# Where the first seed copies and the exponential's table load stand, and how far ahead seeds are loaded, in a two-headed SSM and attention kernel

## The chip, the cores and the metric

One Trainium2 chip, one core. The metric is the device time of one execution in microseconds, and the comparison is between the kernel before and the kernel after the change.

## The reference

Two independent heads on sequences of 2048 positions and width 448 are computed and put side by side. Head A is a long convolution with a diagonal state-space kernel; head B is softmax attention with 16 heads of width 28.

```python
# A: S4D convolution
dt = exp(log_dt);  A = -exp(log_A_real) + 1j * A_imag
C = (C_real + 1j * C_imag) * dt[:, None]
P = exp((A * dt[:, None])[:, :, None] * pos)      # 448 x 256 x 2048
K = 2 * einsum("dn,dnl->dl", C, P).real
a = irfft(rfft(u_t, 2L) * rfft(K, 2L))[:L] + u * D_skip
# B: attention, 16 heads of 28
q, k, v = split(x @ wqkv)
p = softmax(q @ k.T * 28 ** -0.5)
b = (p @ v).reshape(S, D) @ wo
out = concatenate([a, b], -1)
```

## The kernel before

The kernel has a prologue, a loop of 256 steps and a tail.

The **prologue** projects x to q, k and v with TensorE (each evacuated into a high and a low part by ACT and DVE, tile `hl`, and written to DRAM) and works out "seeds" for the state-space kernel: low powers of the complex exponentials, from which all 2048 positions are later built by multiplication. Seeds need ACT's sine and exponential functions, which lie in different tables, so the program has table loads (`ACT_TABLE_LOAD` in the profile) between them. Seeds are written to DRAM (`sd`). In the prologue a planner is free to order the instructions of each engine. At its end the scores' maxima of attention unit 0 are found, in 16 groups of 4 (`max_mm`, line 173).

One group of `max_mm` takes four products of 128 x 512 scores on TensorE (tiles `pm`). The first is passed through a relu on ACT (tile `rl`), the second is joined with it on DVE (custom instruction, output `rl`), the third and fourth are reduced on DVE (output `mx`). `max_end` and `max_put` (lines 198 and 206) turn the maxima over and write them as two further rows into the tile `qhat`, through which they come into the scores.

The **loop** runs over 16 units (4 groups of 4 heads, 4 chunks of 512 queries each) with 16 key tiles each. A step (`ORDER`, line 34) holds four score products with their exponentials on ACT (`s_mm`, tiles `pss` and `p`), the previous step's four products with v (`pv_step`, tile `po`), one group of maxima for a coming unit (19 steps ahead: 16 and `LEAD` = 3), and pieces of the convolution. In the loop and from line 861 on, every engine's instructions, SP's DMA requests among them, stay in the order in which the program writes them.

The pieces of the convolution that matter here are the 56 **blocks** of 8 channels, one each 3.5 steps. For a block b:

- `load_sd(b)` (line 615) loads its seeds into a tile `sdb`, 128 x 672 floats;
- `k_seeds(b)` (line 619) copies them on ACT, at its first call into the tile `e`, at its second into `g`;
- `k_start(b)` copies further factors into `zg`; `e_power` (line 633) then doubles the powers in `e` in nine instructions on POOL, `g_powers` those in `g` on DVE;
- `k_mm` (line 674) multiplies e by g on TensorE, four steps after the block began.

The next load is issued by `k_next` (line 987) once a block's powers have all been written into the program. Between prologue and loop stand the loads and copies for block 0 and then the first `LEAD` groups of maxima for unit 1.

Of the kernel before, what the change touches and what calls it, by code (L numbers as in the profile page):

```python
# [8 lines left out]
F32 = mybir.dt.float32  # L9
F32R = mybir.dt.float32r  # L10
I32 = mybir.dt.int32
AF = mybir.ActivationFunctionType
# [38 lines left out]
NB = D // 8  # L51
# [7 lines left out]
SDF = F_Z + 18 * 16  # L59
# [31 lines left out]
def body(ctx, tc, a, out):  # L91
    nc = Engines(tc)
# [4 lines left out]
    def pool(stack, name, bufs=1, space=None, side=None):  # L97
        kw = {} if space is None else {"space": space}
        if side:
            kw["side"] = side  # L100
        return stack.enter_context(tc.tile_pool(name=name, bufs=bufs, reuse_waits="tile", **kw))
# [71 lines left out]
    def max_mm(u, i, kc, ps=w_tile):  # L173

        if i == 0 and kc == 0:
            m_u[u] = q_p.tile([128, HG, 4, 3], F32, name="mx", bufs=2)
        j, t = divmod(i, 4)
        pm = ps()
        q, kt = q_u[u][:, j, t * 128:(t + 1) * 128], kt_g[u // NQ][j]
        mx = m_u[u][:, j, t, max(kc - 1, 0):max(kc - 1, 0) + 1]  # L180
        if kc == 0:
            nc.tensor.matmul(pm, q, kd_g[u // NQ, j], start=True, stop=True)
            rl_u[u, i] = kd_p.tile([128, CQ], F32, name="rl", bufs=2)
            nc.scalar.activation(rl_u[u, i], pm, AF.Relu)
        elif kc == 1:
            kb = kt.rearrange("p (c s n) -> p c s n", c=NQ, s=2)[:, :2, 1, :]
            nc.tensor.matmul(pm.rearrange("p (c n) -> p c n", c=2), q, kb, start=True, stop=True)
            rl = rl_u.pop((u, i))
            nc.vector.tensor_tensor_reduce(rl, pm, rl, 1.0, -3.0e38, ALU.add, ALU.max, mx)
        else:  # L190
            nc.tensor.matmul(pm, q, kt[:, kc * CQ:(kc + 1) * CQ], start=True, stop=True)
            nc.vector.tensor_reduce(mx, pm, axis=AX.X, op=ALU.max)

    def max_join(u):
        m_u[u, 1] = q_p.tile([128, HG * 4], F32, name="m1", bufs=2)
        nc.vector.tensor_reduce(m_u[u, 1], m_u[u].rearrange("p a b c -> p (a b) c"), axis=AX.X, op=ALU.max)

    def max_end(u, ps):
        nc.tensor.transpose(ps[:16, :128], m_u[u, 1], ident)
        mh = q_p.tile([16, 2, 128], F32R, name="mh")  # L200
        nc.vector.tensor_scalar(mh[:, 0, :], ps[:16, :128], -1.0, None, op0=ALU.mult)
        nc.vector.scalar_tensor_tensor(mh[:, 1, :], ps[:16, :128], -1.0, mh[:, 0, :].bitcast(F32),
                                       op0=ALU.mult, op1=ALU.subtract)
        mh_u[u] = mh
# [7 lines left out]
    with ExitStack() as st:  # L212
# [54 lines left out]
        half_pi = s_p.tile([128, 1], F32, name="half_pi")  # L267
# [276 lines left out]
        for i in range(16):  # L544
            for kc in range(4):
                max_mm(0, i, kc, more[(4 * i + kc) % 5])
        max_join(0)
        max_end(0, ps_t.tile([128, CQ], F32, name="pt"))
        max_put(0)
# [6 lines left out]
    g_p = pool(g_st, "g_p")  # L556
# [56 lines left out]
    sds, egs = {}, {}  # L613

    def load_sd(b):
        sds[b] = g_p.tile([128, SDF], F32, name="sdb", bufs=3)
        nc.sync.dma_start(sds[b], sd_d[b // BO][b % BO])

    def k_seeds(b):

        if b not in es:
            es[b] = e = g_p.tile([128, 2, 16, N2], F32, name="e", bufs=2)
            nc.scalar.activation(e[:, :, :, :8], sds[b][:, :F_G].rearrange("p (c h e) -> p c h e", c=2, e=8), AF.Copy)
        else:
            g = g_p.tile([128, 2, 16, N1], F32, name="g", bufs=2)
            nc.scalar.activation(g[:, :, :, :4], sds[b][:, F_G:F_Z].rearrange("p (c h e) -> p c h e", c=2, e=4), AF.Copy)
            egs[b] = es.pop(b), g
# [231 lines left out]
        return spectrum(f, i, p, uh_p, ps, b0) if kind == "s" else finish(f, i, p, ps, b1)  # L859

    nc.kept = KEPT["a"]
    load_sd(0)
    load_sd(1)
    k_seeds(0)
    k_seeds(0)
    for i in range(LEAD):
        for kc in range(4):
            max_mm(1, i, kc)

    urgent, back = collections.deque(), collections.deque()  # L870
    powers = {"g": collections.deque(), "e": collections.deque()}
# [113 lines left out]
    last = [None]  # L985

    def k_next():

        if last[0] is not None and not powers["e"] and not powers["g"]:
            if last[0] + 2 < NB:  # L990
                load_sd(last[0] + 2)
            last[0] = None

    def vec():
# [4 lines left out]
    for s in range(NS):  # L999
# [26 lines left out]
        for op in ORDER:  # L1026
            if op[0] == "s":
                ps.append(s_mm(u, kt, int(op[1])))
            elif op[0] == "f":
                slot(s)  # L1030
            elif op[0] == "v":
                vec()
            elif op == "k":
                k_next()
                k_begin(s)
                k_seed(s)
                for _ in range(3):
                    if powers["e"]:
                        powers["e"].popleft()()
            elif op == "pv":  # L1040
                if prev:
                    pv_step(*prev)
                    if prev[1] == NK - 1:
                        fin(prev[0], s)
            elif sm < NS:
                max_mm(sm // NK, sm % NK, int(op[1]))
        for _ in range(FX if late[0] else 0):
            slot(s)
        if sm < NS and sm % NK == NK - 1:
# [3 lines left out]
            max_join(sm // NK)  # L1053
            soon_slot(UG[0], end)
        k_next()
        prev = (u, kt, ps)
    pv_step(*prev)
# [65 lines left out]
```

## Time and profile before

| what | value |
|---|---|
| median of 3 runs | 1332.18 us (1330.11 to 1336.95) |
| the profiled execution | 1331.76 us, span 1329.9 us |
| mean granted TensorE clock | 0.975 |
| busy share of the span | TensorE 93%, DVE 74%, ACT 72%, POOL 63% |

The span is the time from the first to the last instruction in the trace; the execution's own time is 1.9 us longer. Busy times of TensorE are modelled, since its products overlap. All instructions of the compute engines carry the line of one helper (L75), so rows are told apart by their tiles: `p<-pss` reads "writes p, reads pss". "SPq" is a request that SP issues, "DMA" the transfer itself.

### The profile page before, as it was taken

The numbers are of one execution on the slowest core, as the hardware profiler recorded it, in microseconds if no ns is written. First come the engines' busy times: TensorE is split into PE (matmuls) and PEld (weight loads), VectorE is DVE, ScalarE is ACT, GpSimd is POOL, SyncE is SP. The second block draws the span as 40 slices with busy tenths as digits, with TensorE's granted clock in tenths as the row PEclk, the third lists the DMA queues.
The fourth block names the chain that finished last, engine by engine and source line by source line (L and its number), as shares of the span: only waits on it lengthen the run. The fifth ranks groups of instructions, "written<-read, shape, count | busy, mean of one in ns | idle before, by whom it ended". The sixth has DMA issues, their size and how long they took to land.

```text
span 1329.9 us, 33195 instructions
## 1 busy us (share of the span) xinstructions
PE 1235.2 (93%) x12625; PEld 705.0 (53%) x12625; DVE 990.1 (74%) x2138; ACT 953.2 (72%) x2067; POOL 838.4 (63%) x704
## 2 busy tenths in 40 slices
PE   6878885699999999999999999999999999898997
PEld 5656763355555555555555555555555545444433
DVE  5897786787777887787788988888886858757311
ACT  4876762388888888888888888888886656555553
POOL 2686681378788788888779999989992202211211
PEclk9989888799999999999999999999999999999999
DMA  6677669725856546468634233732415553825485
GB/s 188 207 272 264 217 211 287 206 57 122 191 134 152 128 129 163 135 165 235 172 95 95 61 72 89 165 78 69 100 50 148 192 157 134 263 102 162 150 217 140
DMA packets 200088, 205.36 MB, mean 154 GB/s; under 512 B 95992, under 2 KB 158520, under 8 KB 197880
## 3 DMA queue, kind: packets, MB, share of 16 engines
q1 hardware_dynamic: 199928, 203.23, 55.1%
q8 instruction: 100, 1.64, 0.5%
q14 instruction: 60, 0.49, 0.1%
HBM read 120.73 MB, written 82.18 MB: 153 GB/s over the span
## 4 chain that ended last, share of the span: by engine, by line
PE 69%; DVE 14%; DMA 5%; ACT 5%; POOL 4%; issue 2%; SPq 1%; ACTq 0%; POOLq 0%; DVEq 0%
PE pm L75 39%; PE pss L75 15%; PE po L75 15%; DVE mx L75 2%; DVE p L75 2%; DVE tri L75 2%; DVE pr L75 1%; POOL qhat L75 1%; ACT p L75 1%; DVE rl L75 1%; DVE sg L75 1%; DVE qhat L75 1%; ACT tri L75 1%; DMA qhat<-q 1%; DVE px L75 1%
## 5 line engine op out<-in xcount | busy, mean ns | idle before, releaser
L75 ACT ACTIVATE p<-pss 128x512 f32<-128x512 f32 x1024 | 561.6, 611 | 118.7 <-PE pss L75 114.3
L75 PE MATMUL pss<-qhat,khat 128*128 128x512 f32 x1024 | 403.3, 400 | 3.8 <-ACT p L75 3.7
L75 DVE TENSOR_REDUCE mx<-pm 128x1 f32<-128x512 f32 x500 | 321.5, 684 | 102.4 <-PE pm L75 100.9
L75 PE MATMUL pm<-khat,qhat 128*128 128x512 f32 x749 | 326.9, 439 | 19.3 <-DVE mx L75 6.7
L75 POOL TENSOR_TENSOR e<-e,sdb 128x256 f32<-128x256 f32 x168 | 201.8, 1201 | 126.7 <-ACT e L75 107.8
L75 PE MATMUL po<-p,v 128*32 128x512 f32 x2048 | 269.9, 596 | 0.0
L75 POOL TENSOR_TENSOR e<-e,eu 128x256 f32<-128x256 f32 x168 | 248.1, 1477 | 13.2
L75 PEld LDWEIGHTS pm<-khat,qhat 128*128 128x128 f32 x749 | 141.5, 189 | 215.1 <-ACT p L75 47.0
L75 DVE CUSTOM_DVE_ANT_0 rl<-pm,rl 128x512 f32<-128x512 f32 x249 | 171.5, 689 | 66.0 <-ACT rl L75 62.2
L75 PEld LDWEIGHTS pss<-qhat,khat 128*128 128x128 f32 x1024 | 190.6, 188 | 50.8 <-ACT p L75 12.4
L75 POOL TENSOR_TENSOR eu<-e,sdb 128x256 f32<-128x256 f32 x168 | 202.0, 1202 | 0.0
L75 POOL TENSOR_TENSOR p<-pr,pr 64x448 f32<-64x448 f32 x32 | 40.9, 1278 | 197.3 <-DVE pr L75 186.3
L75 DVE TENSOR_TENSOR g<-g,zg 128x128 f32<-128x128 f32 x392 | 162.1, 414 | 4.0 <-ACT zg L75 0.6
L75 ACT ACTIVATE rl<-pm 128x512 f32<-128x512 f32 x249 | 151.1, 607 | 16.8 <-PE pm L75 16.8
L75 PE MATMUL pm<-xh,khat 112*128 112x512 f32 x256 | 92.3, 444 | 21.3 <-DVE hl L75 9.8
L75 PE MATMUL pm<-kdif,qhat 128*128 128x512 f32 x249 | 100.9, 405 | 2.3 <-DVE mx L75 1.3
L75 DVE TENSOR_TENSOR zg<-g,zg 128x128 f32<-128x128 f32 x224 | 87.9, 392 | 5.1
L75 PEld LDWEIGHTS pm<-e,g 128*32 128x32 f32 x3584 | 57.6, 110 | 44.0 <-issue 17.8
L75 PE MATMUL pm<-e,g 128*32 128x64 f32 x3584 | 73.7, 222 | 1.9 <-POOL e L75 1.9
L75 ACT ACTIVATE y<-pm 128x448 f32<-128x448 f32 x48 | 26.3, 549 | 65.9 <-issue 32.8
L75 PEld LDWEIGHTS pm<-xh,khat 112*128 112x128 f32 x256 | 53.4, 213 | 36.6 <-DVE hl L75 11.2
L75 PEld LDWEIGHTS po<-p,v 128*32 128x32 f32 x2048 | 55.8, 110 | 22.4 <-issue 17.9
(134 smaller groups left out, 1503.9 us busy)
## 6 DMA issues: line engine op xcount, KB each, us to landing
sdb<-sd SPq DMA_DIRECT2D x56, 336.0 KB
khat<-k SPq DMA_DIRECT2D x64, 256.0 KB
qhat<-q SPq DMA_DIRECT2D x64, 256.0 KB
sd<-sg SPq DMA_DIRECT2D x8, 1456.0 KB
k<-hl SPq DMA_DIRECT2D x16, 512.0 KB
q<-hl SPq DMA_DIRECT2D x16, 512.0 KB
mw<-in_mw SPq DMA_DIRECT2D x16, 512.0 KB
sd<-qhat SPq DMA_DIRECT2D x8, 896.0 KB
```

What stands on the lines that cost most here:

```text
L75: i = f(*args, **kw)
```

## The change

Three edits:

1. The first copies of seeds (both calls of `k_seeds(0)`) stand behind the `LEAD` groups of maxima ahead of the loop, not in front of them.
2. A one-element exponential on ACT is written behind the maxima of unit 0 in the source. It is in the part that the planner orders, and it reads and writes only the constant that the last sine used. In the built program it stands, with the table load in front of it, behind the last six `sg` copies of the seeds and ahead of an `hl` copy; the table load ahead of the loop's first `p` is no longer in the program.
3. Seeds are loaded three blocks ahead, in four tiles, instead of two ahead in three. Three loads stand in front of the loop, and in the loop the load of block b+3 stands where that of block b+2 stood.

Other than these, and the fourth tile's effect on where the later tiles of the same pool lie, every engine's order is as before.

```diff
@@ -544,6 +544,7 @@
         for i in range(16):
             for kc in range(4):
                 max_mm(0, i, kc, more[(4 * i + kc) % 5])
+        nc.scalar.activation(half_pi[:1], half_pi[:1], AF.Exp)
         max_join(0)
         max_end(0, ps_t.tile([128, CQ], F32, name="pt"))
         max_put(0)
@@ -613,7 +614,7 @@
     def load_sd(b):
-        sds[b] = g_p.tile([128, SDF], F32, name="sdb", bufs=3)
+        sds[b] = g_p.tile([128, SDF], F32, name="sdb", bufs=4)
         nc.sync.dma_start(sds[b], sd_d[b // BO][b % BO])
@@ -859,13 +860,13 @@
     nc.kept = KEPT["a"]
-    load_sd(0)
-    load_sd(1)
-    k_seeds(0)
-    k_seeds(0)
+    for b in range(3):
+        load_sd(b)
     for i in range(LEAD):
         for kc in range(4):
             max_mm(1, i, kc)
+    k_seeds(0)
+    k_seeds(0)
@@ -987,8 +988,8 @@
     def k_next():
         if last[0] is not None and not powers["e"] and not powers["g"]:
-            if last[0] + 2 < NB:
-                load_sd(last[0] + 2)
+            if last[0] + 3 < NB:
+                load_sd(last[0] + 3)
             last[0] = None
```

## The prediction

> **What bounds the kernel now.** I read the page first, then the busy times by stage, then the chain of waits around the start of the loop, and last the single instructions of each engine there.
>
> ```profile
> span 1329.9 us, 33195 instructions
> ...
> PE 69%; DVE 14%; DMA 5%; ACT 5%; POOL 4%; issue 2%; SPq 1%; ACTq 0%; POOLq 0%; DVEq 0%
> ```
>
> The chain that ended last runs over TensorE for two thirds of the span. By stage (columns: stretch, length, busy us and instruction count of PE, PEld, DVE, ACT, POOL, then granted clock, DMA share, GB/s):
>
> ```profile
> 225.00:250.00 25.00, 18.81 (x46) 8.55 (x46) 21.78 (x49) 5.97 (x10) 0.00 (x0) 0.91 0.91 254
> 250.00:300.00 50.00, 44.94 (x375) 23.01 (x376) 37.34 (x87) 36.27 (x78) 37.11 (x31) 0.91 0.38 90
> 600.00:800.00 200.00, 197.33 (x2372) 110.15 (x2372) 165.00 (x393) 167.12 (x388) 172.50 (x137) 1.00 0.47 121
> 800.00:1000.00 200.00, 199.22 (x2409) 113.91 (x2408) 175.24 (x421) 169.93 (x385) 185.05 (x146) 1.00 0.39 93
> ```
>
> The reader is to see two regimes. In the loop TensorE is busy nearly without a break (199.22 of 200), at the full clock, with POOL second (185.05). Just ahead of it, from 225 to 300, TensorE has holes and the granted clock is 0.91. All three edits act on that seam, so what they are worth is read there. The chain of waits across it (start, length, what):
>
> ```profile
> 248.44 0.29 DVE mh L75
> ...
> 249.75 3.07 DMA sdb<-sd
> ...
> 253.30 0.29 ACT g L75
> ...
> 254.13 5.85 PE pm L75 x10
> ...
> 260.85 1.06 issue
> 261.91 0.61 ACT p L75
> ```
>
> The last maximum of unit 0 is ready at 248.7. Then the chain goes not through work but through a transfer: the first seeds (sdb) are requested at 249.75 and are there at 252.82, ACT copies them (the row at 253.30), and only then do the maxima of unit 1 go on. A second hole follows, 1.06 us of "issue" ahead of the first exponential p at 261.91. The instructions behind the two holes, TensorE first and then ACT (a bracket gives the idle time before, and what ended it):
>
> ```profile
> 238.75 0.79 PE L75 MATMUL pm<-kdif,qhat 128*128 128x512 f32 x1 [1.30 <-DVE mx L75]
> ...
> 248.06 0.47 PE L75 MATMUL pm<-kdif,qhat 128*128 128x512 f32 x1
> ...
> 254.13 0.79 PE L75 MATMUL pm<-khat,qhat 128*128 128x512 f32 x1 [5.14 <-ACT rl L75]
> ...
> 259.47 0.50 PE L75 MATMUL pm<-kdif,qhat 128*128 128x512 f32 x1
> ...
> 262.56 0.50 PE L75 MATMUL pss<-qhat,khat 128*128 128x512 f32 x1 [0.93 <-ACT p L75]
> ```
>
> ```profile
> 252.98 0.42 ACT L75 ACTIVATE e<-sdb 128x256 f32<-128x256 f32 x1 [8.57 <-DMA sdb<-sd]
> ...
> 253.50 0.58 ACT L75 ACTIVATE rl<-pm 128x512 f32<-128x512 f32 x1
> ...
> 260.00 0.60 ACT L75 ACTIVATE rl<-pm 128x512 f32<-128x512 f32 x1 [1.40 <-PE pm L75]
> 260.62 1.28 ACT L75 ACT_TABLE_LOAD   x1
> 261.91 1.08 ACT L75 ACTIVATE p<-pss 128x512 f32<-128x512 f32 x2
> ```
>
> TensorE had unit 1's first product finished at 248.53 (248.06 + 0.47), but ACT, in order, stood at the copy e<-sdb until 252.98 with the product's relu (rl, at 253.50) queued behind it. TensorE has three buffers there, filled them and stood 5.14 us. The second hole is the table load at 260.62, between rl and the first p.
>
> **Part 1: the copies behind the maxima.** In the built program's order ACT now has three rl, then e and g, then the loop's first rl. At the loop's start rl follows its product by 0.03 us (259.47 + 0.50, then 260.00), so the first rl comes at 248.56 instead of 253.50: **−4.94 us**. The two following groups are paced by DVE:
>
> ```profile
> 254.11 0.69 DVE L75 CUSTOM_DVE_ANT_0 rl<-pm,rl 128x512 f32<-128x512 f32 x1 [5.39 <-ACT rl L75]
> ...
> 256.41 0.69 DVE L75 CUSTOM_DVE_ANT_0 rl<-pm,rl 128x512 f32<-128x512 f32 x1 [0.40 <-ACT rl L75]
> ...
> 258.71 0.69 DVE L75 CUSTOM_DVE_ANT_0 rl<-pm,rl 128x512 f32<-128x512 f32 x1 [0.40 <-ACT rl L75]
> ...
> 260.71 0.69 DVE L75 CUSTOM_DVE_ANT_0 rl<-pm,rl 128x512 f32<-128x512 f32 x1
> ```
>
> The intervals are 2.30, 2.30 and 2.00 us: the first two with products of 0.79 us (slow clock, after the 5.14 us of standing) and 0.40 us of DVE idle, the third with a product of 0.50 us and none. With no standing ahead of them I take 2.00 for all: **−0.60 us**. The ends are −0.80 (the two idle times of 0.40 go altogether) and 0 (the clock drops anyway: at 238.75 a product took 0.79 after an idle of only 1.30). [...]
>
> The copies still have to go somewhere. The third rl would start at 248.56 + 2 x 2.00 = 252.56 and end at 253.16, by which time the load has landed (252.82). Both copies take 0.52 us (252.98 to 253.50), so they end at 253.68, and the loop's first rl is due at 248.56 + 3 x 2.00 = 254.56. They lie in 0.88 us of free ACT time: 0. If that cover goes because the third load, now requested with the first two, shares their bandwidth, the landing is at worst half as late again (3.07 x 1.5, at 254.36) and that rl slips by some 0.5 us.
>
> **Part 2: the exponential's table.** The load leaves the place at 260.62. Its worth is between the 0.93 us that TensorE stood for that p (row at 262.56) and 1.29 (p at 260.62 instead of 261.91); I take the chain's own piece, **−1.06 us**. In the built order it stands with a one-element exponential behind the last six sg copies, ahead of an hl copy of the projections. Around that place (ACT, DVE, SP, TensorE, and two stages):
>
> ```profile
> 195.52 1.22 ACT L75 ACTIVATE sg<-sg 128x112 f32<-128x112 f32 x6
> 196.63 0.68 ACT L75 ACTIVATE hl<-pm,kones 128x512 fp32r<-128x512 f32 x1
> ...
> 197.45 0.74 DVE L75 SCALAR_TENSOR_TENSOR hl<-pm,kones,hl 128x512 fp32r<-128x512 f32 x1
> ...
> 198.96 0.39 SPq L75 DMA_DIRECT2D k<-hl  x1
> ...
> 215.10 0.77 PE L75 MATMUL pt<-kdif,qhat 128*128 128x512 f32 x1 [11.49 <-DMA qhat<-q]
> ...
> 203.00:206.00 3.00, 0.61 (x3) 0.17 (x1) 0.12 (x1) 0.69 (x1) 2.84 (x4) 1.00 1.07 309
> ```
>
> The copy is late by 1.28 + at most 0.3 (the 128-element g at 253.30 takes 0.29): 1.58. Its DVE half ends at 198.19, SP sends the write at 198.96, so 0.77 of that is slack and the write is late by 0.8. What waits on it is a stage in which the DMA engines are full (share 1.07) and TensorE stands 11.49 us for qhat: a request 0.8 us late joins a backlog that is cleared no later. I take **+0.2**, between 0 and 1.58. That cover is the point to watch: if the backlog were shorter the load would just have been moved along the same path.
>
> [...]
>
> **Part 3: seeds three blocks ahead.** The sum of loads is unchanged; one moves up in front of the u loads.
>
> ```profile
> sdb<-sd SPq DMA_DIRECT2D x56, 336.0 KB
> ACT e L75 <- DMA sdb<-sd: 11.5, 6, 8.6
> 478.21 0.42 ACT L75 ACTIVATE e<-sdb 128x256 f32<-128x256 f32 x1 [1.15 <-DMA sdb<-sd]
> ```
>
> Of the 11.5 us that ACT ever waited for seeds, 8.6 is the wait that Part 1 removes. The other five total 2.9, the longest 1.15 at 478. In the loop no such wait shows up as an idle TensorE, so I take **0**, with −2.9 as the other end. The tile for block b+3 with four tiles is that of block b−1, just as b+2 was with three: SP's wait for POOL's last reading stays what it was, as do the loads queued behind it.
>
> **Sum.** −4.94 − 0.60 − 1.06 + 0.2 = −6.4 on the profiled execution's 1331.76 (span 1329.9 plus 1.9 around it): 1325.4. The median of the runs shown is 1332.18, 0.4 above; 1325.4 is also within their scatter (1330.11 to 1336.95) of that. The shift should carry to the end, since behind the seam every queue is in order and waits on work, not on a clock. One engine does not shift: POOL starts its first powers when the copy e is done.
>
> ```profile
> 253.47 0.62 POOL L75 TENSOR_TENSOR e<-e,sdb 128x256 f32<-128x256 f32 x1 [46.67 <-ACT e L75]
> ...
> 262.93 2.39 POOL L75 TENSOR_TENSOR e<-e,eu 128x1024 f32<-128x1024 f32 x1
> ...
> 274.50 0.65 PE L75 MATMUL pm<-e,g 128*32 128x64 f32 x32
> ...
> 697.96 0.65 PE L75 MATMUL pm<-e,g 128*32 128x64 f32 x32 [1.27 <-POOL e L75]
> POOL e L75 <- ACT e L75: 107.8, 28, 46.7
> ```
>
> A block takes POOL 11.85 us (253.47 to 265.32). With the copy at 253.16 instead of 252.98 its first block ends at 265.5; TensorE will ask for it at 274.50 − 6.4 = 268.1. The margin shrinks from 9.2 to 2.6 us but stays.
>
> **The rivals.** *POOL sets the pace.* POOL starts no earlier, and if it paces the loop (185.05 of 200, and TensorE waited 1.27 us for e at 697.96) the lead is given back block by block until nothing is left: 1331.8. Against: apart from the first 46.7, POOL waited 61.1 us for ACT's copies in 27 places, so it catches up again and again. Chance 0.09.
>
> *The table load is only moved.* If the 1.58 us stay on the prologue's path: 1331.76 − 4.94 − 0.60 − 1.06 + 1.58 = 1326.7, and 1327.3 if the clock also stays down. For: the hl copy stands on the way to the last transfers; against: the 11.49 us wait at full DMA share. Chance 0.15.
>
> *The loop's seed waits count too*: 2.9 more, 1322.5. For: ACT is in order and its p feed TensorE. Against: TensorE never shows them. Chance 0.08.
>
> *Slower: the new places of POOL's tiles.* The fourth tile moves e, g and eu in memory. If POOL's products took longer there, the loop would fall to POOL's pace. 56 blocks of 11.85 are 664 us; POOL has 61.1 to spare and the 6.4 won, so it decides from 10% on. At 12% it is 80 − 68 = 12 us more than before, 1344. For: POOL is the second busiest engine. Against: nothing in the trace shows its times depending on place. Chance 0.07.
>
> **How the numbers follow.** The forecast, −6.4, has 0.61. A measurement of this kernel can tell about 0.5%, 6.66 us, from no change, and the forecast lies almost on that line. Its own range is 1322.5 to 1328 (prologue 0 to 1.58, clock 0 to −0.80, table 0.93 to 1.29, runs that scatter); I put 0.38 of its 0.61 beyond the line, because the loop's seed waits can only add, and 0.23 within. Faster: 0.38 + 0.08 = 0.46. Within: 0.23 + 0.15 + 0.09 = 0.47. Slower: 0.07. The range reaches from the largest gain, 1322.0, less the 1.65 by which the fastest run lay under the profiled one, 1320.4, to the rival that gives all back, 1331.8; it leaves out the slower rival and the edges.
>
> **What would show it.** Right: in the profile after, rl of unit 1 starts at about 248.8 with no wait for sdb ahead of it; its DVE intervals are 2.0; no table load stands between rl and p, and p starts near 255.5; TensorE's waits of 5.14 and 0.93 are gone; loop rows are otherwise as before, earlier by 6.4. Wrong: TensorE's first pt of the maxima later than 215.3 (the load was only moved); TensorE waiting for POOL's e near 268 or through the loop; p-to-p steps in the loop longer than before; or an e copy that still waits for its load with rl behind it.

## The result, and the profile after

The changed kernel takes 1324.73 us (median of 7 runs, 1321.28 to 1325.35), the kernel before 1331.34 (7 runs, 1328.70 to 1336.95): a ratio of 0.9931, 95% interval 0.9913 to 0.9948. The forecast was 1325.4. The profiled execution took 1324.82. From its page:

```profile
span 1323.0 us, 33194 instructions
...
PE 69%; DVE 15%; POOL 5%; ACT 4%; issue 3%; DMA 2%; SPq 0%; ACTq 0%; POOLq 0%; DVEq 0%
```

The span is 6.9 us shorter (1329.9 before), and transfers went from 5% to 2% of the chain that ended last. By stage:

```profile
225.00:250.00 25.00, 19.57 (x48) 8.95 (x47) 22.58 (x52) 6.58 (x11) 0.00 (x0) 0.91 0.94 261
250.00:300.00 50.00, 49.87 (x437) 26.75 (x436) 39.99 (x92) 39.19 (x88) 42.69 (x35) 0.94 0.44 107
```

From 250 to 300 TensorE is now busy 49.87 of 50 us instead of 44.94; late in the loop nothing has changed (199.23 of 200 from 800 to 1000, 199.22 before). ACT across the seam, and in the prologue where the table load now stands:

```profile
196.79 1.28 ACT L75 ACT_TABLE_LOAD   x1
198.09 0.20 ACT L75 ACTIVATE half_pi<-half_pi 1x1 f32<-1x1 f32 x1
198.20 0.66 ACT L75 ACTIVATE hl<-pm,kones 128x512 fp32r<-128x512 f32 x1
...
248.67 0.60 ACT L75 ACTIVATE rl<-pm 128x512 f32<-128x512 f32 x1 [4.14 <-PE pm L75]
...
253.18 0.60 ACT L75 ACTIVATE rl<-pm 128x512 f32<-128x512 f32 x1 [1.69 <-PE pm L75]
253.67 0.41 ACT L75 ACTIVATE e<-sdb 128x256 f32<-128x256 f32 x1
...
255.48 0.60 ACT L75 ACTIVATE rl<-pm 128x512 f32<-128x512 f32 x1 [1.20 <-PE pm L75]
255.97 1.15 ACT L75 ACTIVATE p<-pss 128x512 f32<-128x512 f32 x2
```

The first rl comes at 248.67 (253.50 before); the copy e follows the third rl and waits for nothing; p starts 0.49 us after the loop's first rl, with no load between.

**How the kernels are compared.** The profiled executions of different kernels begin unit 0's maxima anywhere from 211.2 to 216.9 us, also where their prologues are alike, and single executions scatter by several us. Lengths within one trace are steadier. I use three marks: m, DVE's last reduction of unit 0's maxima; p, ACT's first exponential; and the twelfth copy `o<-po`, which ends unit 11. Their rows, before and then after (p of both is shown already):

```profile
247.47 0.20 DVE L75 TENSOR_REDUCE m<-mx 128x16 f32<-128x48 f32 x1
995.08 0.73 ACT L75 ACTIVATE o<-po 128x512 f32<-128x512 f32 x1
```

```profile
247.57 0.20 DVE L75 TENSOR_REDUCE m<-mx 128x16 f32<-128x48 f32 x1
988.02 0.72 ACT L75 ACTIVATE o<-po 128x512 f32<-128x512 f32 x1
```

So the seam, m to p, took 261.91 − 247.47 = 14.44 us before and 8.40 after; the loop, p to the end of unit 11, 733.17 and 732.05. All kernels, worked out in the same way from the same rows of each (the times that a ratio compares were taken beside runs of the kernel before on the same chip):

| kernel | seam, us | loop, us | median, us | ratio to before (95%) |
|---|---|---|---|---|
| before | 14.44 | 733.17 | | |
| after | 8.40 | 732.05 | 1324.73 | 0.9931 (0.9913 to 0.9948) |
| after, again | 8.40 | 732.10 | 1323.39 | 0.9927 (0.9914 to 0.9940) |
| copies alone | 9.82 | 733.34 | 1327.38 | 0.9955 (0.9942 to 0.9968) |
| table alone | 13.49 | 733.68 | 1331.88 | 0.9986 (0.9972 to 1.0000) |
| lead alone | 14.47 | 732.58 | 1330.43 | 0.9983 (0.9971 to 0.9996) |
| copies and table | 8.40 | 733.74 | 1325.76 | 0.9949 (0.9934 to 0.9963) |
| copies and table, again | 8.40 | 736.14 | 1327.06 | 0.9951 (0.9934 to 0.9967) |
| four tiles, lead two | 8.69 | 733.84 | 1324.52 | 0.9938 (0.9923 to 0.9953) |
| lead four | 8.40 | 731.03 | 1323.08 | 0.9929 (0.9913 to 0.9944) |
| copies split | 11.06 | 731.70 | 1326.58 | 0.9949 (0.9938 to 0.9961) |
| TensorE kept busy | 7.51 | 731.47 | 1323.76 | 0.9927 (0.9914 to 0.9940) |
| three table loads | 8.39 | 731.82 | 1325.54 | 0.9941 (0.9921 to 0.9961) |
| POOL held back | 8.01 | 737.61 | 1326.65 | 0.9949 (0.9927 to 0.9970) |

### The profile page after: what moved, and what is told of

It reads as the page before. It is cut to its first block, busy times and chain, and to the rows that moved or that the text cites. A ratio compares the mean times of both kernels' runs of the same rounds, so it can differ in the third digit from the quotient of the medians.

```text
span 1323.0 us, 33194 instructions
## 1 busy us (share of the span) xinstructions
PE 1235.2 (93%) x12625; PEld 705.6 (53%) x12625; DVE 989.7 (75%) x2138; ACT 953.3 (72%) x2068; POOL 839.9 (63%) x704
## 4 chain that ended last, share of the span: by engine, by line
PE 69%; DVE 15%; POOL 5%; ACT 4%; issue 3%; DMA 2%; SPq 0%; ACTq 0%; POOLq 0%; DVEq 0%
PE pm L75 39%; PE po L75 15%; PE pss L75 15%; DVE mx L75 3%; DVE tri L75 2%; DVE p L75 2%; DVE pr L75 2%; DVE rl L75 1%; POOL e L75 1%; POOL qhat L75 1%; DVE qhat L75 1%; ACT tri L75 1%; DVE sg L75 1%; DVE px L75 1%; ACT p L75 1%
## 5 line engine op out<-in xcount | busy, mean ns | idle before, releaser
L75 POOL TENSOR_TENSOR e<-e,sdb 128x256 f32<-128x256 f32 x168 | 202.2, 1203 | 118.0 <-ACT e L75 108.8
```

The lines of the kernel that those rows point to most:

```text
L75: i = f(*args, **kw)
```

## The experiments

**The three edits one at a time.** Copies alone:

```diff
-    k_seeds(0)
-    k_seeds(0)
     for i in range(LEAD):
         for kc in range(4):
             max_mm(1, i, kc)
+    k_seeds(0)
+    k_seeds(0)
```

> Only the copies e and g are moved behind the three groups of maxima of unit 1; table load and seed loads as before. Theory of head-of-line blocking on ACT (copies wait for the seeds' transfer, rl behind them): the first rl of unit 1 starts at about 248.6 instead of 253.5 and e no longer delays it; the table load still stands between the loop's first rl and p; TensorE still works at half clock for these groups, as in the changed kernel. The shift at the first p is then about -4.9 + 0.4 = -4.5 us, and the time 1331.8 - 4.5 = 1327.3. The forecast's working (intervals of 2.00 us): -5.5, 1326.2. Rival (the transfer's wait just moves on to the loop, since e is still needed by the POOL): no shift left at the end of the loop, 1331.8.

The seam fell by 4.62 us, to 9.82, and the lead is still there at the end of the loop: ratio 0.9955. With 1333.60 for before that is 6 us (4 to 8), against 4.5 expected and nothing by the rival; the seam's 4.62 lies inside that interval. The load still stands between rl and p:

```profile
254.04 0.41 ACT L75 ACTIVATE e<-sdb 128x256 f32<-128x256 f32 x1
...
255.85 0.60 ACT L75 ACTIVATE rl<-pm 128x512 f32<-128x512 f32 x1 [1.20 <-PE pm L75]
256.46 1.28 ACT L75 ACT_TABLE_LOAD   x1
257.76 1.09 ACT L75 ACTIVATE p<-pss 128x512 f32<-128x512 f32 x2
```

Table alone:

```diff
+        nc.scalar.activation(half_pi[:1], half_pi[:1], AF.Exp)
         max_join(0)
```

> Only the one-element exponential in the prologue, so that the table load stands there. Theory: p follows rl by 0.5 us instead of 1.9, -1.4 us at the first p, and the maxima of unit 0 start no later than 0.1 us (215.2 instead of 215.1), since the hl copy's delay of some 1.5 us ends in a backlog of transfers: 1330.4. The forecast: -1.06 + 0.2, 1330.9. Rival (the load is only moved): the start of the maxima 1.5 us later, end unchanged, 1331.8.

The seam fell by 0.95 us alone, and by 1.42 (9.82 to 8.40) on top of the copies. p does follow rl by 0.49 us in both, instead of 1.91: the load's own worth is 1.42 in both. Alone, rl itself came later: the seeds' copy started 0.17 us later behind m than before, and the slow clock lasted through the loop's first group as well (0.30 us). The ratio's interval touches 1.

```profile
248.78 0.42 ACT L75 ACTIVATE e<-sdb 128x256 f32<-128x256 f32 x1 [8.76 <-DMA sdb<-sd]
...
256.10 0.60 ACT L75 ACTIVATE rl<-pm 128x512 f32<-128x512 f32 x1 [1.70 <-PE pm L75]
256.59 1.17 ACT L75 ACTIVATE p<-pss 128x512 f32<-128x512 f32 x2
```

Lead alone (`bufs=4`, three loads ahead of the loop, `last[0] + 3`), and the other two without it:

> Only the lead of the seed loads: three blocks ahead in four tiles, copies and table as before. The forecast: 0, 1331.8. Theory from the two traces: at the ends of the units the shift grows by 0.55 us in unit 1, 0.4 in unit 3, 0.3 in unit 5 and is 1.4 in all, at the units in which ACT had waited for seeds (2.9 us in five waits): 1330.4, with no wait of ACT for seeds left but the first one of 8.6 us. Rival (the 1.4 come from the earlier start, another phase of transfers against work): no shift at the ends of the units, 1331.8.

> Copies and table as in the changed kernel, seeds two blocks ahead in three tiles as before. Theory: -4.4 at the copies, -1.4 at the table, together -5.7 from the first unit's end on, and no further step in the units with waits for seeds: 1326.1; ACT still waits for seeds in the loop, some 2.9 us in all. Rival (the phase of transfers, not the lead, gave the last 1.4): -7.1 at the loop's end, 1324.7.

The expectation read steps at single units (1, 3 and 5) as the lead's; these kernels do not repeat those steps in these sizes, so that reading falls. What remains is the loop as a whole: 732.58 with lead three, 733.74 with lead two, and a ratio of 0.9983 for the lead alone, whose interval leaves out 1. One wait for seeds is left with the lead alone (first row), four and three in two executions without it:

```profile
ACT e L75 <- DMA sdb<-sd: 8.6, 1, 8.6
```

```profile
ACT e L75 <- DMA sdb<-sd: 2.8, 4, 1.1
```

**Lead or tile?** The changed kernel and "copies and table" once more on one chip, then two that vary the lead with the tiles:

> The changed kernel once more, beside the same kernel with seeds two ahead in three tiles and others. It carries edit 3 on top of that one: the forecast expects no difference from it (the waits removed cost TensorE nothing), the rival 1.4 to 2.9 us less. From the last maximum of unit 0 (m) to the first p: 8.4 us, as in its first profile.

> Copies and table as in the changed kernel, seeds two ahead in three tiles, on the same chip as the changed kernel: the same time within 1 us by the forecast, 1.4 to 2.9 us more by the rival. From m to the first p 8.4 us.

```diff
-    for b in range(3):
-        load_sd(b)
+    load_sd(0)
+    load_sd(1)
...
-            if last[0] + 3 < NB:
-                load_sd(last[0] + 3)
+            if last[0] + 2 < NB:
+                load_sd(last[0] + 2)
```

> The changed kernel with the seeds' four tiles kept and the lead taken back to two blocks. From the first p to the end of unit 11 kernels with lead two took 733.2 to 736.1 us and those with lead three 731.5 to 732.6. Theory (the lead counts, since ACT no longer waits for seeds): 733.2 or more, with waits for seeds of 3 to 4 us in the loop. Rival (the fourth tile counts, by its places in memory or the freedom to load): 732.6 or less.

> The changed kernel with seeds four blocks ahead in five tiles. Theory (a lead of three already removes all waits for seeds in the loop): from the first p to the end of unit 11 the same 731.5 to 732.6 us, the time as the changed kernel's. Rival (more lead gives the loop more freedom): under 731.5.

Ordered by lead, the loops separate without overlap at this mark. Lead two, six executions: 733.17, 733.34, 733.68, 733.74, 733.84, 736.14. Lead three, six (POOL held back left out): 731.47 to 732.58. Lead four, one: 731.03. Four tiles with lead two lie with lead two, and wait for seeds again:

```profile
ACT e L75 <- DMA sdb<-sd: 4.8, 5, 1.8
```

(This kernel's slow stretch reaches 1.6 us into the loop, which costs unit 0 some 0.5 us; without that it is still 733.3.) So the lead counts, by about 1.5 us on average and more where the transfers are late (the 736.14). At the end of unit 15 one lead-two execution (copies and table, 1045.4 us behind p) lies inside the range of lead three (1044.5 to 1046.1); the other five lie above it. The ratios alone would not settle it, 0.9927 against 0.9951 with intervals that overlap.

The traces also show how the wait reaches TensorE. All six executions with lead two wait for seeds near 149 and 217 us behind p, 0.5 to 1.8 us each time, and by the fourth copy `o<-po` they are 255.0 to 256.3 us behind p, those with lead three 254.0 to 254.3. In the kernel before, the wait of 1.15 us at 478.21 that the forecast shows is followed by this one on TensorE:

```profile
479.17 0.49 PE L75 MATMUL pss<-qhat,khat 128*128 128x512 f32 x1 [0.23 <-ACT p L75]
```

In "copies and table, again" the same place costs ACT 1.81 us and TensorE 0.88. Lead four lies 0.4 us under the shortest of lead three, which the theory had not expected and one execution cannot decide; its ratio is no better than the changed kernel's.

**Does the order on ACT make the wait?** The copies behind the first of the three groups:

```diff
     for i in range(LEAD):
         for kc in range(4):
             max_mm(1, i, kc)
-    k_seeds(0)
-    k_seeds(0)
+        if i == 0:
+            k_seeds(0)
+            k_seeds(0)
```

> The changed kernel with the two copies of block 0's seeds behind the first of the three groups of maxima instead of behind the third. Theory (ACT in order: whatever stands behind the copy waits until the seeds' transfer lands, 5.3 us after m): the first rl at m + 1.1 as in the changed kernel, the second at m + 6 instead of m + 3.3, so from m to the first p 11 us instead of 8.4, and 2.7 us more in all. Rival (the earlier start of the first group is all that counts, TensorE's three buffers cover the rest): 8.4 and no difference.

```profile
246.77 0.60 ACT L75 ACTIVATE rl<-pm 128x512 f32<-128x512 f32 x1 [4.34 <-DVE mh L75]
251.06 0.42 ACT L75 ACTIVATE e<-sdb 128x256 f32<-128x256 f32 x1 [3.69 <-DMA sdb<-sd]
...
251.58 0.58 ACT L75 ACTIVATE rl<-pm 128x512 f32<-128x512 f32 x1
```

The seam is 11.06 us, as expected (11). The second rl stands behind a copy that waits 3.69 us for the transfer. The loss follows the place in the queue, and the ratio does too: 0.9949, against 0.9927 for the changed kernel on that chip.

**The clock at the seam.** The forecast had the three groups run at full clock once the stall of 5.14 us was gone. They do not; DVE and TensorE of the changed kernel:

```profile
249.30 0.69 DVE L75 CUSTOM_DVE_ANT_0 rl<-pm,rl 128x512 f32<-128x512 f32 x1 [0.48 <-ACT rl L75]
...
251.59 0.69 DVE L75 CUSTOM_DVE_ANT_0 rl<-pm,rl 128x512 f32<-128x512 f32 x1 [0.40 <-ACT rl L75]
...
253.89 0.69 DVE L75 CUSTOM_DVE_ANT_0 rl<-pm,rl 128x512 f32<-128x512 f32 x1 [0.40 <-ACT rl L75]
...
256.34 0.69 DVE L75 CUSTOM_DVE_ANT_0 rl<-pm,rl 128x512 f32<-128x512 f32 x1 [0.55 <-PE pm L75]
```

```profile
247.92 0.27 PE L75 MATMUL pt<-ident,m 128*16 128x128 f32 x1 [2.23 <-DVE m L75]
...
249.32 0.80 PE L75 MATMUL pm<-khat,qhat 128*128 128x512 f32 x1 [0.22 <-ACT rl L75]
```

The intervals are 2.29, 2.30 and 2.45 us and a product takes 0.80. In slices of 1 us (the granted clock is the third number from the end):

```profile
248.00:249.00 1.00, 1.00 (x4) 0.48 (x3) 0.56 (x2) 0.33 (x1) 0.00 (x0) 1.00 0.06 19
249.00:250.00 1.00, 0.78 (x2) 0.29 (x1) 0.70 (x3) 0.27 (x1) 0.00 (x0) 0.56 0.04 8
...
253.00:254.00 1.00, 1.00 (x3) 0.69 (x3) 0.60 (x2) 0.82 (x3) 0.00 (x0) 0.50 0.97 272
...
256.00:257.00 1.00, 1.00 (x6) 0.75 (x4) 0.66 (x3) 1.00 (x3) 0.92 (x2) 1.00 0.32 75
```

The clock halves at about 249, though TensorE had just begun to work again, and is back by 256. What lies ahead is 2.23 us in which TensorE waited for DVE to finish unit 0's maxima. The kernel before has the same wait, and there too the clock had halved by 249, when the stall of 5.14 us (254.13 − 5.14 = 248.99) was only beginning:

```profile
247.82 0.27 PE L75 MATMUL pt<-ident,m 128*16 128x128 f32 x1 [2.23 <-DVE m L75]
```

```profile
249.00:250.00 1.00, 0.00 (x0) 0.00 (x0) 0.00 (x0) 0.00 (x0) 0.00 (x0) 0.50 0.04 8
```

By the clock records of the changed kernel's trace the clock changes at 238.87, 242.28, 249.11 and 255.94, by those of the kernel before at 238.73, 242.14, 248.97 and 259.21: the steps are 3.41, 6.83 and 6.83 us, and 3.41, 6.83 and 10.24, all whole multiples of 3.41. In the 3.41 us ahead of 249.11 (245.69 to 249.11, the idle window of the theory that follows) TensorE was busy for 1.18 us. To test whether the wait does it, I gave TensorE something to do there:

```diff
+        nc.kept = ("tensor",)
+        warm = ps_n.tile([128, CQ], F32, name="pn")
+        for i in range(8):
+            nc.tensor.matmul(warm, q_u[0][:, 3, 384:512], kt_g[0][3][:, 1536:], start=True, stop=True)
+        nc.kept = KEPT["p"]
         max_join(0)
```

> The changed kernel with eight products more, which nothing reads, on TensorE between the last product of unit 0's maxima and the turning of the maxima, where it stood idle for 2.2 us. Theory: the granted clock is decided in windows of some 3.4 us, and the idle window of 245.7 to 249 is why the three groups of unit 1 run at half clock; with it filled, the products take 0.5 instead of 0.8 us, the intervals of DVE's rl 2.0 instead of 2.3, and from m to the first p it takes 7.2 us instead of 8.4: 1323.5 beside the changed kernel's 1324.7. Rival (light work of the groups themselves lowers the clock): 8.4, and no difference in time, or up to 0.3 us more where the added products run late.

```profile
246.35 2.00 PE L75 MATMUL pn<-khat,qhat 128*128 128x512 f32 x8
...
250.14 0.51 PE L75 MATMUL pm<-khat,qhat 128*128 128x512 f32 x1 [0.22 <-ACT rl L75]
```

```profile
250.12 0.69 DVE L75 CUSTOM_DVE_ANT_0 rl<-pm,rl 128x512 f32<-128x512 f32 x1 [0.47 <-ACT rl L75]
...
252.12 0.69 DVE L75 CUSTOM_DVE_ANT_0 rl<-pm,rl 128x512 f32<-128x512 f32 x1
...
254.13 0.69 DVE L75 CUSTOM_DVE_ANT_0 rl<-pm,rl 128x512 f32<-128x512 f32 x1
...
256.13 0.69 DVE L75 CUSTOM_DVE_ANT_0 rl<-pm,rl 128x512 f32<-128x512 f32 x1
```

```profile
250.00:251.00 1.00, 0.63 (x2) 0.31 (x2) 0.88 (x3) 0.09 (x1) 0.00 (x0) 1.00 0.04 8
```

The intervals are 2.00, 2.01 and 2.00 us, the product takes 0.51, the clock stays at 1.00 though TensorE is busy for only 0.63 of this slice (so the rival, light work of the groups, falls), and the seam is 7.51 instead of 8.40 (7.2 expected). Eight products that nothing reads shorten the seam by 0.9 us. In the times this does not show (ratio 0.9927, as for the changed kernel on that chip).

This is one execution with the filler. In all thirteen without it the clock fell to 0.50, between 0.1 us before m and 1.5 us behind it, for 3.4, 6.8, 10.2 or 13.7 us (in two pieces of 3.4 with the copies split). With the changed kernel's order on ACT the seam follows that length: 8.01 us with 3.4 (POOL held back), 8.39 to 8.40 with 6.8, 8.69 with 10.2 (four tiles, lead two). The length of a wait alone does not decide: the wait of 1.30 us that stands ahead of the row at 238.75 in the kernel before is in all fourteen traces, and the clock fell at it in seven of them.

**The table load in the prologue.** Two loads more at its place:

```diff
         nc.scalar.activation(half_pi[:1], half_pi[:1], AF.Exp)
+        nc.scalar.activation(half_pi[:1], half_pi[:1], AF.Sin, scale=0.1)
+        nc.scalar.activation(half_pi[:1], half_pi[:1], AF.Exp)
```

> The changed kernel with two more table loads at the place in the prologue (a one-element sine and an exponential more): one hl copy is then some 3 us later than without any, the next some 4.4. From the last six sg copies to the first product of unit 0's maxima kernels with no load there took 19.5 to 19.7 us, those with one 19.6 to 19.8. Theory (a backlog of transfers covers the place): under 21 us, since only what exceeds the slack of the write is passed on. Rival (each load is passed on in full): 22.5, and the time 3 us more.

```profile
196.01 1.22 ACT L75 ACTIVATE sg<-sg 128x112 f32<-128x112 f32 x6
197.25 1.28 ACT L75 ACT_TABLE_LOAD   x1
...
198.76 1.28 ACT L75 ACT_TABLE_LOAD   x1
...
200.85 1.28 ACT L75 ACT_TABLE_LOAD   x1
...
206.08 0.69 ACT L75 ACTIVATE hl<-pm,kones 128x512 fp32r<-128x512 f32 x1 [3.26 <-DMA k<-hl]
...
216.04 0.77 PE L75 MATMUL pt<-kdif,qhat 128*128 128x512 f32 x1 [9.80 <-DMA qhat<-q]
```

From the sg copies to the first product of the maxima it is 20.03 us with three loads, 19.63 with one and 19.58 with none. The third hl takes up the delay by waiting less for its transfer (3.26 us, 6.68 with no load). Of 4.4 us put on ACT (three loads and their one-element activations), 0.4 come through. The load was not merely moved.

**How much POOL can be late.** In the changed kernel its first block ended at 266.08 and TensorE took it up at 268.78. Five additions of `sdb` to itself, ahead of block 0's powers:

```diff
     k_seeds(0)
     k_seeds(0)
+    dum = g_p.tile([128, SDF], F32, name="dum")
+    for i in range(5):
+        nc.gpsimd.tensor_tensor(dum, sds[0], sds[0], ALU.add)
```

> The changed kernel with five additions of the first seeds to themselves on POOL (128 x 672, by the neighbouring shapes 1.3 us each) ahead of block 0's powers; nothing reads what they write. They hold POOL's first block back by some 5.5 us. Theory (margin): in the changed kernel POOL's first block ended 2.7 us before TensorE asked for it, so TensorE waits 2.8 us for e at the first product e,g and the loop up to the end of unit 11 takes 2.8 us more at most; from the second block on POOL has margin again. Rival (POOL sets the pace of the loop): the whole 5.5 us, 1330.

```profile
252.96 6.84 POOL L75 TENSOR_TENSOR dum<-sdb 128x672 f32<-128x672 f32 x5 [44.86 <-DMA sdb<-sd]
```

```profile
271.65 0.93 PE L75 MATMUL pm<-e,g 128*32 128x64 f32 x32 [3.58 <-POOL e L75]
...
276.75 0.65 PE L75 MATMUL pm<-e,g 128*32 128x64 f32 x32
```

```profile
272.00:273.00 1.00, 1.00 (x28) 0.56 (x22) 0.00 (x0) 0.37 (x2) 0.92 (x3) 0.50 0.00 0
...
276.00:277.00 1.00, 1.00 (x20) 0.59 (x22) 0.93 (x4) 1.00 (x4) 1.00 (x1) 1.00 0.00 0
```

POOL began 5.6 us later (259.76 instead of 254.16) and the loop took 5.5 us more (737.61 against 732.10), the rival's number and twice the theory's. But the place is the theory's: there is one long wait of 3.58 us, at block 0, and after it the clock is halved for 3.4 us. The product e,g takes 0.93 instead of 0.65 there. Most of the loop's 5.5 us is lost by the end of unit 0 (5.2, from p to the first `o<-po`). POOL does not pace the loop; the wait was larger than the margin said, since p came 0.7 us earlier in this execution, and it cost its clock besides: 3.58 and half of 3.4 make 5.3. That is one trace. The eight times scatter from 1321.99 to 1330.27 (the profiled one is 1329.34), and their ratio, 0.9949 against 0.9927 to 0.9931 for the changed kernel, is 2.4 to 2.9 us with intervals that overlap; by the times, the theory's 2.8 stands as well as 5.5.

## Why the prediction was right

The time, the way and the size were right: 1325.4 forecast, 1324.73 measured. That the sum came out so near is in part luck: the clock term had the wrong sign, and the table and the lead gave more than forecast and made up for it. By the marks of the two profiled executions, the copies gave −4.93, the slow groups +0.31 and the table −1.42, together the 6.04 us of the seam (6.6 forecast); up to m it was +0.10, in the loop to unit 11 −1.12 (0 forecast) and behind it +0.2, in all −6.9. The +0.10 is chance, since m lay anywhere from 243.1 to 249.3 in the fourteen traces.

- **Copies, −4.94: right.** From m the first rl came after 6.03 us before and 1.10 after, −4.93. The copy e started at 253.67 instead of 253.16 and held up nothing, as the free ACT time said.
- **Clock, −0.60: wrong.** The step that failed is "with no standing ahead of them I take 2.00 for all". DVE's intervals stayed at 2.3 and the third grew to 2.45; on ACT, from the first rl to the loop's first, it took 6.81 us instead of 6.50: 0.31 more, not 0.60 less. The forecast put the slow products down to the stall, but the clock halved as the stall began (249.0), and the idle stretch before m was still there in the changed kernel. Whether the stall alone would have slowed the groups is not shown. That closing it gives the 0.60 was the author's estimate, and no run shows it: all three intervals at 2.00 (2.00, 2.01 and 2.00) came only with the eight products in the idle stretch. The row at 238.75, from which the forecast took its end of 0, was the better guide to this change: a wait of 1.30 us stood ahead of the slow clock there, and one of 2.23 us here, where the slow stretch lasted 6.83 us (249.11 to 255.94).
- **Table, −1.06: mis-sized.** From rl to p it took 1.91 us with the load between and 0.49 or 0.50 without: 1.42 less, where 1.29 was the upper end. With the load gone, p also lost the short gap between rl and the load, since rl and p then overlap on ACT (255.48 + 0.60 ends after 255.97). The 0.95 of the table alone lies within the bounds only because the copies and the slow clock took 0.47 back. The load itself took 1.28 us (196.79 in the changed kernel), and the next activation started 0.02 after it (198.09).
- **Prologue, +0.2: right in kind, 0.05 in size.** The cover was a backlog of transfers, and it holds for three loads too. The rival "only moved" falls.
- **Lead, 0: mis-sized.** It is worth 1 to 2 us of the 2.9 given as its other end. "TensorE never shows them" was the step that failed: behind the very wait that the forecast shows, TensorE stood 0.23 us for p, and in the first 700 us from p it was busy for 694.43 before and 695.59 after. The rival "the loop's seed waits count too" was right in kind, and its 2.9 too large: ACT's wait of 1.15 us reached TensorE as 0.23.
- **POOL's margin, 2.6 forecast: 2.7 measured.** The rival that POOL sets the pace falls: TensorE waited for POOL's e in two places, 1.9 us in all, before and after alike. What a late POOL costs beyond its wait rests on one trace.
- **The range.** Its largest gain, 1322.0, leaves out the clock term's own end of −0.80; with it the sum is 1321.8. Nothing hangs on this.
- **Slower by the tiles' new places: did not happen.** POOL's products `e<-e,sdb` (of three widths, 168 in all) average 1203 ns in the profile after, 1201 before.

## What to carry to other kernels

Ahead of a loop, look for an instruction that waits on a transfer in front of work that is ready on the same in-order queue; move it behind that work. The gain is the time by which that work then starts earlier, less what is still late behind it. Put a table load where a backlog of transfers covers it, and test that with several more loads at the place. Where single waits are too small to see on the engine that bounds a loop, compare the loop's length between marks over several traces: run times alone scattered by more than the effect.

## What was not expected of the hardware

An idle TensorE cost twice here: 2.2 us of waiting ahead of m left the next products at half clock until 256, and in one trace a wait of 3.58 us in the loop cost about 5.2. Every slow stretch at the seam lasted 3.4 us or a whole multiple of it, and at the same wait of 1.30 us the clock fell in seven traces of fourteen and stayed up in the others. Eight products without a reader in the idle stretch kept the clock at full, and the seam went from 8.40 to 7.51 us. The kernels with that filler and with lead four have the shortest loops seen (731.47 and 731.03 us, the next 731.70), but neither is faster than the changed kernel by a measured time (0.9927 and 0.9929 against 0.9927 to 0.9931).
